# An expert unit for the first four batches' tokens, run in pieces between attention's last steps

## The chip, the cores and the metric

One core of one Trainium2 chip. The metric is device time in microseconds of one execution. TensorE (PE) multiplies, VectorE (DVE) does the top-k search and two-operand arithmetic, ScalarE (ACT) copies, exponentials and signs, GpSimd (POOL) additions and the indirect transfers, SyncE (SP) issues most of the other transfers. Each engine works through its own instructions in the order in which the program wrote them.

## The reference, cut to what matters

```python
scores = q @ k.T / 8                              # 8 batches x 8 heads, 576 x 576, head size 64
kth    = the 32nd largest score of each row
attn   = softmax(where(scores >= kth, scores, -1e9))
x      = (attn @ v) as 4608 tokens x 512          # all heads of a token side by side
e(n)   = argmax(x[n] @ w_gate)                    # one of 8 experts for each token
out[n] = prob(e(n)) * (relu(x[n] @ w1[e]) @ w2[e])  # 512 -> 1024 -> 512
```

## The kernel before

**Attention** runs in 144 steps (`steps`), a step being two 128-row slots of scores. The loop over `t` (lines 1004 to 1078) is a software pipeline: step t makes the scores of slot t+3 (`scores`, `scores_left`, PE and ACT, into the bank pair `MAINS` and one of seven SBUF buffers that `pair()` hands out), finds the top 32 of slot t (`topk`, lines 1025 and 1033, DVE: 21 first-level MAX8 and some 14 second-level operations), marks and adds (`softmax`, lines 454 and 455: ACT's sign, POOL's addition) slot t-2, transposes slot t-3 (`transp`, line 461), takes the exponential of slot t-4 (`exps`) and multiplies slot t-5 by the values (`av`, line 477). From t = 144 on the pipeline only empties; there are seven such steps.

**Side work** stands in lanes of generators (`j_sums`, `j_rows`, `j_find`, `j_redo`, `j_patch`, `j_route`): scaling and storing finished rows, repairing rows whose 32nd place is tied, and routing each batch's tokens into a table by expert. `advance` moves each lane by one `yield`; what a job emits goes into queues that are written out right after (DVE's at the next step, where the loop is still in attention). There is one `advance` in each attention step, one in each of the steps 144 to 148 (`TAIL`, `TADV = 5`, line 1061), and later one per expert layer (`drain(g)`, line 1425). A batch's chain is find, redo, patch, route, one `yield` after the other; the last batch's starts at t = 145.

**Experts.** An expert's tokens are worked in units of `T` tiles of 128 tokens. A unit has 8 layers `k` of 128 hidden values (`FC`). A layer is `hidden` (12 matmuls, line 1159, each operand split into a high and a low part, hence three products) and `project` (3 matmuls per tile, line 1174). Its weights (512 KB) are loaded by `raw_w` (lines 946 and 947) and split by `parts_w` into high (ACT line 954, DVE line 956) and low parts (DVE and POOL, line 957). A unit's tokens are gathered by `take` (line 876) and transposed and split by `turn_x` (line 1139 PE, 1140 ACT, 1141 DVE). `EARLY` names units that may run before all batches are routed: expert 0 with two tiles of tokens of the first five batches, experts 1 to 4 with three tiles of the first six. Then come experts 5 to 7 with five tiles each, what is left of experts 0 to 4 (three tiles, and four times two), and a spare tile. In `moe` step k, `fetch(u + 1)` gathers the next unit's tokens as soon as its batches are routed, and one tile is turned after each of a unit's layers 3 to 7. A unit whose tokens need all batches (`u >= first`) is fetched only once all lanes are empty, after which the counting of leftover tokens (`over`, lines 1242 to 1271) runs with a `moe` step between its parts.

**Around the border.** At t = 140 the first two layers' weights are loaded into the query and key buffers (`ahead_load`), at t = 145 unit 0's tokens are gathered (`ahead_take`), at t = 146 the two layers are split (`ahead_split`). All of unit 0's matmuls come after step 150.

Of the kernel before, what the change touches and what calls it, by code (L numbers as in the profile page):

```python
# [24 lines left out]
A0, A1, A2, A3 = -4, 1, 2, 2  # L25
EARLY = ((4, 1, 2), (3, 4, 3))
# [13 lines left out]
TADV = 5  # L40
# [8 lines left out]
def attention_moe(ctx, tc, q, k, v, w_gate, w1, w2, out):  # L49
    nc = tc.nc  # L50
# [738 lines left out]
    def j_route(b):  # L789
# [52 lines left out]
        for c in range(KB):  # L842
            if c == 0 or b not in ahead:
                yield need(pool=1.0)
# [104 lines left out]
    def parts_w(k, tiles):  # L949
        W[k] = []  # L950
        for i, r in enumerate(RAW.pop(k)):
# [5 lines left out]
            (nc.gpsimd if i else nc.vector).tensor_tensor(lo, r, hi, op=OP.subtract)  # L957
# [3 lines left out]
    def ahead_load(k):  # L961
        r = work.tile([128, MAIN, 4, D], F32, name=("rq", "rk")[k], bufs=1).rearrange("p i g d -> p (i g d)")
        raw_w(k, r[:, 0:DM], r[:, DM:2 * DM])

    def ahead_take():
        c, T = part_of[0]
        GX[0] = [jobs.tile([128, DM], F32, name="kt", bufs=4)[:, 0:DM] for _ in range(T)]
        for i in range(T):
            take(GX[0][i], ID[0][:, i, 0:1], c)

    def ahead_split(k):
        if k == 0:
            for i in range(2):
                t = jobs.tile([128, 2, VW], F32R, name=f"rv{(NQ + i) % NV}", bufs=1).rearrange("p g x -> p (g x)")
                SPARE.extend(t[:, c * DM:(c + 1) * DM] for c in range(2 * VW // DM))
            SPARE.extend(jobs.tile([128, DM], F32, name="kt", bufs=4).bitcast(F32R)[:, 0:DM] for _ in range(2))
        parts_w(k, [SPARE.pop(0) for _ in range(4)])

    SPARE = []
# [17 lines left out]
    if NQ > 1:  # L997
# [3 lines left out]
    AHEAD = [(A0, ahead_load, (0,)), (A0, ahead_load, (1,)), (A1, ahead_take, ()), (A2, ahead_split, (0,)),  # L1001
             (A3, ahead_split, (1,))]
    delayed = None
    for t in range(steps + LAG + TD + 4):
# [60 lines left out]
        for at, job, a in AHEAD if first else ():  # L1065
            if t - steps == at:
                job(*a)
# [14 lines left out]
    while first and part_of[0][0] not in ROUTED or held[0]:  # L1082
# [9 lines left out]
    late = {}  # L1092
    XP, HT, PY = {}, {}, {}
    outs = []

# [30 lines left out]

    def turn_x(u, t):
        T = units[u][2]
        if t >= T:
# [367 lines left out]
```

## Time and profile before

| | |
|---|---|
| median of 3 runs | 1301.82 us (1299.66 to 1303.17) |
| the profiled execution: its own time, its span | 1301.19 us, 1299.4 us |
| mean granted TensorE clock | 0.983 |
| busy PE, DVE, ACT, POOL | 1217.2, 1020.2, 828.3, 830.7 us |
| PE instructions, DVE instructions | 9126, 6889 |
| last top-k block ends, first expert layer begins | 760, 787.4 us |
| first five-tile unit begins | 969.7 us |

The page is read from the 40 slices of part 2: slices 1 to 23 are attention, in which DVE is at 9 tenths or more nearly throughout; slices 24 and 25 hold the border; from slice 26 on PE is at 9 nearly throughout and DVE falls to 3 to 7. "Granted clock" is TensorE's clock as a share of 2.4 GHz; it has two levels, so a share between one half and one is a mix over time of 1.2 and 2.4 GHz. Matmul ends are modelled, so that a busy PE need not be PE at its best.

### The profile page before, as it was taken

To read this page: it belongs to the slowest core of one execution; us is meant where nothing else is said; L and a number is where in the kernel's file an instruction comes from. 1 tells how busy PE (TensorE), PEld (TensorE's weight loads), DVE (VectorE), ACT (ScalarE), POOL (GpSimd) and SP (SyncE) were. 2 spreads that over 40 slices of the span, in tenths; PEclk is the share of its full clock that TensorE was granted. 3 is DMA by queue.
4 is the path that set the end of the run, shared out by engine and by line. 5 is a ranking of instruction groups with operands and counts; after the bars stand their busy time and mean duration, and the time that the engine had idled before them with its cause. 6 is when DMAs were issued, how large, how long until landed. Compare 5 with 4: busy or idle time off the path is not lost.

```text
span 1299.4 us, 31672 instructions
## 1 busy us (share of the span) xinstructions
PE 1217.2 (94%) x9126; PEld 968.9 (75%) x9126; DVE 1020.2 (79%) x6889; ACT 828.3 (64%) x1691; POOL 830.7 (64%) x1205
## 2 busy tenths in 40 slices
PE   6999999999999999999998869999999999999997
PEld 3667667676666666667666658889899899989996
DVE  7999999999999999999998965746663333345664
ACT  4999798898888888888987843333332323233432
POOL 4676766867867867868957866676552424155654
PEclk8999999999999999999999978999999999999999
DMA  6765565655655656556653615646563434256774
GB/s 174 224 184 178 169 187 161 186 171 160 193 161 156 195 168 171 179 170 171 188 166 113 194 39 159 187 122 199 146 184 110 125 93 132 74 162 189 224 212 125
DMA packets 271239, 211.18 MB, mean 163 GB/s; under 512 B 136216, under 2 KB 214216, under 8 KB 271056
## 3 DMA queue, kind: packets, MB, share of 16 engines
q1 hardware_dynamic: 260320, 185.92, 48.2%
q0 software_dynamic: 9504, 22.86, 5.6%
q8 instruction: 74, 1.21, 0.4%
q14 instruction: 109, 0.89, 0.2%
q10 hardware_dynamic: 1232, 0.30, 0.1%
HBM read 102.49 MB, written 107.90 MB: 162 GB/s over the span
## 4 chain that ended last, share of the span: by engine, by line
DVE 43%; PE 43%; ACT 4%; issue 3%; POOL 3%; DMA 2%; SPq 1%; POOLq 0%; ACTq 0%; DVEq 0%
DVE cand L1025 21%; PE ph L1159 18%; PE y L1174 17%; DVE cand L1033 9%; DVE vq L1033 7%; PE pt L265 2%; ACT sg L454 2%; POOL sb L455 2%; PE mt L1139 1%; PE ps L367 1%; PE px L477 1%; PE tt L461 1%; DVE xm L265 1%; ACT et L467 1%; DMA rk<-in_k_dram 1%
## 5 line engine op out<-in xcount | busy, mean ns | idle before, releaser
L455 POOL TENSOR_TENSOR sb<-sb,sg 128x576 f32<-128x576 f32 x288 | 369.4, 1299 | 49.4 <-ACT sg L454 42.3
L1025 DVE MAX8 cand<-sb 128x8 f32<-128x52 f32 (+2 forms) x3024 | 368.3, 207 | 0.2 <-issue 0.2
L957 POOL TENSOR_TENSOR wl<-r,wh 128x512 fp32r<-128x512 f32 x110 | 142.4, 1294 | 220.8 <-DVE wh L956 213.5
L454 ACT ACTIVATE sg<-sb,nb 128x576 int8<-128x576 f32 x288 | 229.0, 795 | 63.0 <-POOL sb L455 63.0
L477 PEld LDWEIGHTS px<-et,rv 128*64 128x64 f32 x2688 | 130.9, 138 | 123.1 <-ACT xt L265 49.4
L1160 ACT ACTIVATE hh<-ph 128x320 fp32r<-128x320 f32 (+3 forms) x136 | 58.2, 428 | 241.6 <-PE ph L1159 240.1
L1033 DVE MAX8 vq<-cand 128x8 f32<-128x22 f32 (+7 forms) x1152 | 200.5, 205 | 0.0
L461 PE MATMUL tt<-turner,sb 128*128 128x128 f32 x1296 | 176.8, 278 | 23.0 <-POOL sb L455 19.9
L367 PE MATMUL ps<-qk 64*128 64x512 f32 (+1 forms) x576 | 184.9, 650 | 4.2 <-ACT sb L369 3.5
L1161 DVE SCALAR_TENSOR_TENSOR hl<-ph,hh 128x320 fp32r<-128x320 f32 (+3 forms) x136 | 65.0, 478 | 151.3 <-ACT hh L1160 151.2
L467 ACT ACTIVATE et<-tt,shift 128x1152 f32<-128x1152 f32 x144 | 178.2, 1238 | 2.6 <-PE tt L461 2.6
L477 PE MATMUL px<-et,rv 128*64 128x128 f32 (+1 forms) x2688 | 164.3, 268 | 14.6 <-ACT xt L265 9.0
L461 PEld LDWEIGHTS tt<-turner,sb 128*128 128x128 f32 x1296 | 147.9, 144 | 34.7 <-POOL sb L455 30.2
L1159 PE MATMUL ph<-xh,wh 128*128 128x320 f32 (+3 forms) x536 | 168.5, 314 | 0.0
L1159 PE MATMUL ph<-xh,wl 128*128 128x320 f32 (+3 forms) x536 | 165.3, 308 | 0.0
L1159 PE MATMUL ph<-xl,wh 128*128 128x320 f32 (+3 forms) x536 | 165.1, 308 | 0.0
L1033 DVE MATCH_REPLACE8 cand<-vq,cand 128x22 f32<-128x22 f32 (+2 forms) x864 | 158.6, 189 | 0.0
L369 ACT ACTIVATE sb<-ps 128x1024 f32<-128x1024 f32 x144 | 149.0, 1035 | 9.4 <-PE ps L367 9.4
L1174 PE MATMUL y<-wh,hh 128*128 128x512 f32 x324 | 127.9, 395 | 1.9 <-ACT yo L1178 1.9
L1174 PE MATMUL y<-wh,hl 128*128 128x512 f32 x324 | 128.3, 396 | 0.0
L1174 PE MATMUL y<-wl,hh 128*128 128x512 f32 x324 | 128.1, 395 | 0.0
L957 DVE TENSOR_TENSOR wl<-r,wh 128x512 fp32r<-128x512 f32 x110 | 95.7, 870 | 11.4 <-ACT wh L954 7.1
(261 smaller groups left out, 2179.3 us busy)
## 6 DMA issues: line engine op xcount, KB each, us to landing
r<-in_moe_w_dram SPq DMA_DIRECT2D x220, 256.0 KB
sc<-sb SPq DMA_DIRECT2D x128, 288.0 KB
sc<-sb SPq DMA_DIRECT2D x128, 256.0 KB
rv<-in_v_dram SPq DMA_DIRECT2D x32, 256.0 KB
xs<-xm SPq DMA_DIRECT2D x16, 512.0 KB
rq<-in_q_dram SPq DMA_DIRECT2D x60, 128.0 KB
rk<-in_k_dram SPq DMA_DIRECT2D x60, 128.0 KB
sc<-sb SPq DMA_DIRECT2D x32, 144.0 KB
```

What stands on the lines that cost most here:

```text
L367: nc.tensor.matmul(MAINS[:, n], qk[:, 0, w], qk[:, 1, 2 * LEFT:], start=True, stop=True)
L369: nc.scalar.activation(bass.AP(EX[-1].tensor, EX[-1].offset, [list(EX[-1].ap[0]), [S + LEFT, 2], [1, M]]), MAINS, AF.Copy)
L454: nc.scalar.activation(upper(SG[i]), SB[u], AF.Sign, bias=nb[:, i, 1:2], accum_out=CNT[b][:, 2 * lt + i:2 * lt + i + 1])
L455: nc.gpsimd.tensor_tensor(SB[u], SB[u], SG[i], op=OP.add)
L461: nc.tensor.matmul(tt[:, c], x[:, c * 128:(c + 1) * 128], ident, start=True, stop=True, is_transpose=True)
L467: nc.scalar.activation(ET[t], three.rearrange("p (c q) -> p c q", c=NB9), AF.Exp, bias=shift[:, t // NT, 0:1], scale=0.125)
L477: yield lambda kb=kb, blk=blk: nc.tensor.matmul(px[h * 64:(h + 1) * 64], block(rv, p % 2, kb if kb < MAIN else MAIN + n, h), et[:, blk, q] ...
L957: (nc.gpsimd if i else nc.vector).tensor_tensor(lo, r, hi, op=OP.subtract)
L1025: one[m][0](*one[m][1])
L1033: f(*a)
L1159: nc.tensor.matmul(ph, a[:, c, :], x[:, c, s], start=(m == 0), stop=(m == len(seq) - 1))
L1174: nc.tensor.matmul(PY[u, t], a[:, s], x, start=(f == 0 and m == 0), stop=(f == FC - 1 and m == 2))
```

## The change

Expert 0's two-tile unit takes tokens of the first four batches instead of five; expert 1's early unit becomes a two-tile one with tokens of five batches, and its leftover unit a three-tile one. Unit 0 no longer runs in `moe`. A generator, `filler`, holds it in 20 pieces. One piece is taken at the end of each of the steps 139 to 143 and two in each of the steps 144 to 150, one ahead of `av` and one behind `transp`; the last after the loop. Weights come in eight 512 KB loads of two layers' w1 or two layers' w2 (`load`), into the query and key buffers in turn, and are split by ACT or DVE and DVE (`split`), 1024 elements per partition at a time, where the kernel before had 512. The splits lie in the three score-operand buffers, two value buffers and score buffers. `hid` uses `MAINS`, `out_of` accumulates all eight layers in it. Unit 1's tokens are gathered in step 149 (or when routed), turned after the loop in the transposes' bank, and its first layer's weights are loaded and split ahead. `moe` starts at unit 1. `advance` now also runs in steps 149 and 150.

```diff
-A0, A1, A2, A3 = -4, 1, 2, 2
-EARLY = ((4, 1, 2), (3, 4, 3))
+A0 = -5
+EARLY = ((5, 1, 2), (4, 1, 2), (3, 3, 3))
...
-TADV = 5
+TADV = 7
...
-            if c == 0 or b not in ahead:
+            if c == 0 or b not in ahead or b == part_of[0][0]:
                 yield need(pool=1.0)
...
+    def ahead_take(u, name, w):
+        c, T = part_of[u]
+        GX[u] = [jobs.tile([128, w], F32, name=name, bufs=4)[:, 0:DM] for _ in range(T)]
         for i in range(T):
-            take(GX[0][i], ID[0][:, i, 0:1], c)
+            take(GX[u][i], ID[u][:, i, 0:1], c)
...
+        def load(j):
+            r = raws[j] = raw(j)
...
+        def split(j):
+            hi, lo = sets[j % 3 if j < FC - 1 else 2]
+            r = raws.pop(j)
+            if j < FC // 2:
+                nc.scalar.activation(hi, r, AF.Copy)
+            else:
+                nc.vector.tensor_copy(hi, r)
+            nc.vector.tensor_tensor(lo, r, hi, op=OP.subtract)
+
+        def hid(k):
...
+            ph = MAINS[:, k % 2, 0:w]
+            seq = [(c, a, x) for c in range(DC) for a, x in ((h1, xh), (h1, xl), (l1, xh))]
+            for m, (c, a, x) in enumerate(seq):
+                nc.tensor.matmul(ph, a[:, c, :], x[:, c, :], start=(m == 0), stop=(m == len(seq) - 1))
+            nc.scalar.activation(hh, ph, AF.Relu)
+            nc.vector.scalar_tensor_tensor(hl_, ph, 0.0, hh, op0=OP.max, op1=OP.subtract)
...
+        load(0)
+        load(1)
+        yield
+        ahead_take(0, "kt", DM)
+        yield
...
+        split(0)
+        load(2)
+        XP[0] = [spare()[:, 0:DC * w].rearrange("p (c x) -> p c x", c=DC) for _ in range(2)]
+        for t in range(T):
+            turn_x(0, t, MAINS[:, t].rearrange("p (c x) -> p c x", c=DC))
+        yield
+        hid(0)
...
+        split(1)
+        load(3)
+        yield
+        hid(1)
+        sets.append((qs[2][:, 0:two], spare()[:, 0:two]))
+        split(2)
+        load(4)
+        yield
+        split(3)
+        load(5)
+        yield
+        for k in range(2, FC):
+            hid(k)
+            if k % 2:
+                split(4 + k // 2 - 1)
+                if k < FC - 1:
+                    load(6 + k // 2 - 1)
+                else:
+                    r = raw(0)
+                    raw_w(FC, r[:, 0:DM], r[:, DM:two])
+            yield
+        for k in range(FC - 1):
+            out_of(k)
+            if k == 3:
+                split(FC - 1)
+            if k == 4:
+                parts_w(FC, [jobs.tile([128, DM], F32, name="kt", bufs=4).bitcast(F32R) for _ in range(2)]
+                        + [t[:, two:two + DM] for t in rv], nc.vector)
+            if k >= 3 and 1 not in GX and part_of[1][0] in ROUTED:
+                ahead_take(1, "xt", S)
+            yield
...
+        for t in range(T):
+            turn_x(1, t, three[:, t * DM:(t + 1) * DM].rearrange("p (c x) -> p c x", c=DC))
+        out_of(FC - 1)
...
+        if t >= steps:
+            next(fills, None)
         if grp(t - LAG - TD - 2):
             av(t - LAG - TD - 2, grp(t - LAG - TD - 2))
...
             transp(t - LAG - TD)
+        if t >= steps:
+            next(fills, None)
...
+        if steps + A0 <= t < steps:
+            next(fills)
...
-    while first and part_of[0][0] not in ROUTED or held[0]:
+    while held[0] or next(fills, fills) is not fills:
...
-        for k in range(K):
+        load_w(FC + 1)
+        load_w(FC + 2)
+        for k in range(FC, K):
...
+            if k == FC:
+                split_w(k + 1)
             split_w(k + 2)
```

## Rows read from the trace of the kernel before

**Rows 1.** The page, part 2: busy tenths of VectorE and the granted clock of TensorE, in 40 slices of 32.5 us.

```profile
DVE  7999999999999999999998965746663333345664
...
PEclk8999999999999999999999978999999999999999
```

**Rows 2.** Busy time by stretch, from the ninth-last attention step to the first five-tile unit (us from the span's start: length, then busy us and instructions of each engine, granted clock, DMA share, GB/s); the last row sums 12 stretches that cover all of it without a gap.

```profile
735.30:757.00 21.70, 15.19 (x170) 12.20 (x171) 21.70 (x187) 16.02 (x29) 16.01 (x25) 1.00 0.40 127
757.00:762.40 5.40, 2.00 (x21) 1.36 (x19) 5.33 (x29) 1.71 (x7) 3.03 (x4) 0.74 0.04 10
762.40:774.90 12.50, 9.37 (x61) 8.38 (x61) 3.16 (x19) 5.73 (x11) 8.56 (x18) 0.64 0.32 88
774.90:785.60 10.70, 8.97 (x69) 6.61 (x67) 5.43 (x9) 3.39 (x6) 9.69 (x15) 0.92 0.19 42
...
787.40:794.90 7.50, 7.25 (x31) 6.66 (x32) 3.07 (x7) 1.81 (x4) 1.29 (x1) 0.58 0.47 140
...
917.30:925.20 7.90, 6.17 (x26) 5.56 (x25) 5.17 (x27) 1.61 (x3) 1.27 (x1) 0.78 0.30 77
...
sum 234.40, PE 215.00 PEld 189.64 DVE 151.07 ACT 89.77 POOL 148.55; mean PE 17.92 PEld 15.80 DVE 12.59 ACT 7.48 POOL 12.38
```

**Rows 3.** VectorE's instructions in order of time around the end of the last two top-k blocks (start, us, engine, line, what; in brackets the idle time before it and its releaser).

```profile
747.18 2.56 DVE L1025 MAX8 cand<-sb 128x8 f32<-128x52 f32 x21
...
753.69 2.56 DVE L1025 MAX8 cand<-sb 128x8 f32<-128x52 f32 x21
...
759.63 0.39 DVE L1033 MAX8 vq<-cand 128x8 f32<-128x88 f32 x2
...
760.50 1.22 DVE L265 TENSOR_TENSOR hist<-oh,valid 128x40 bf16<-128x40 f32 x1
```

**Rows 4.** TensorE's instructions in order of time from there to the first expert layer, those that it waited for.

```profile
761.77 0.23 PE L265 MATMUL pt<-hist,before 128*128 128x40 bf16 x1 [3.05 <-DVE hist L265]
...
770.45 1.97 PE L477 MATMUL px<-et,rv 128*64 128x128 f32 x16 [3.13 <-ACT r_et L265]
...
787.40 0.58 PE L1159 MATMUL ph<-xh,rv 128*128 128x256 f32 x1 [0.74 <-ACT xh L1140]
```

**Rows 5.** GpSimd's instructions in order of time, at attention's last steps.

```profile
743.26 0.28 POOL L265 IOTA pay<- 128x8 int32 x2
...
760.25 2.50 POOL L455 TENSOR_TENSOR sb<-sb,sg 128x576 f32<-128x576 f32 x2
...
770.95 1.09 POOL L876 DMA_INDIRECT kt<-xs,ids  x1 [0.16 <-issue]
```

**Rows 6.** The chain of waits late in the run, merged (start, us, what): one layer of a three-tile unit and one of a two-tile unit.

```profile
1174.20 2.09 PE ph L1159 x12
1176.29 2.10 PE y L1174 x9
...
1187.54 1.42 PE ph L1159 x12
1188.96 1.40 PE y L1174 x6
```

**Rows 7.** Single lines of code: operations by engine with the duration in ns, min/median/max, and the first and last start; then, from the DMA issues, the median us from issue to landing in the last column.

```profile
L957 DVE TENSOR_TENSOR wl<-r,wh x110: 680/693/2526, 791.9 to 1286.2; 128x512 fp32r<-128x512 f32 x110
L1140 ACT ACTIVATE xh<-mt x40: 582/599/602, 786.3 to 1261.1; 128x512 fp32r<-128x512 f32 x40
L1141 DVE TENSOR_TENSOR xl<-mt,xh x40: 677/692/695, 786.9 to 1261.8; 128x512 fp32r<-128x512 f32 x40
L1161 DVE SCALAR_TENSOR_TENSOR hl<-ph,hh x136: 276/492/558, 791.4 to 1289.8; 128x320 fp32r<-128x320 f32 x48, 128x256 fp32r<-128x256 f32 x40, 128x384 fp32r<-128x384 f32 x40, 128x128 fp32r<-128x128 f32 x8
gx<-xs,ids POOLq DMA_INDIRECT x39, 4.4
kt<-xs,ids POOLq DMA_INDIRECT x2, 3.4
```

**Rows 8.** VectorE and GpSimd in order of time, one moment at which both read two SBUF operands.

```profile
863.63 1.30 POOL L957 TENSOR_TENSOR wl<-r,wh 128x512 fp32r<-128x512 f32 x1
...
863.77 1.70 DVE L957 TENSOR_TENSOR wl<-r,wh 128x512 fp32r<-128x512 f32 x1
```

**Rows 9.** GpSimd in order of time at the end of routing: the last scatter to the table, a weight part, and the first gather of the five-tile unit.

```profile
914.61 0.92 POOL L847 DMA_INDIRECT table<-pay,pos  x1 [0.16 <-issue]
...
925.80 1.29 POOL L957 TENSOR_TENSOR wl<-r,wh 128x512 fp32r<-128x512 f32 x1 [7.06 <-DVE wh L956]
...
931.84 0.99 POOL L876 DMA_INDIRECT gx<-xs,ids  x1
```

**Rows 10.** TensorE there: the count of tokens (line 1441, as in rows 7), and the chain of waits (start, us, what): layer 29's two halves, the first transposes of the five-tile unit, its first layer.

```profile
L1441 PE MATMUL mt<-hist,ones x1: 174/174/174, 918.7 to 918.7; 128*128 128x8 bf16 x1
...
919.37 3.41 PE ph L1159 x12
922.78 2.42 PE y L1174 x9
...
950.74 0.44 PE mt L1139 x4
...
969.71 3.52 PE ph L1159 x24
```

**Rows 11.** TensorE in order of time: the one wait between the first unit and the second.

```profile
824.82 0.50 PE L1174 MATMUL y<-wh,hh 128*128 128x512 f32 x1 [1.91 <-ACT yo L1178]
```

More of the change, by code (lines that the diff above doesn't have):

```diff
@@ L956, in parts_w @@
                 nc.vector.tensor_copy(hi, r)
[L957 removed]
+            ((other or nc.gpsimd) if i else nc.vector).tensor_tensor(lo, r, hi, op=OP.subtract)
             W[k] += [w.rearrange("p (c f) -> p c f", c=DC) if i == 0 else w for w in (hi, lo)]
[L961 to L963 removed]
@@ L979, in attention_moe, with give, turn_x @@
-    SPARE = []
+    late = {}
+    XP, HT, PY = {}, {}, {}
+    outs = []
+    def give(u, t, y):
+        nc.gpsimd.memset(spacer, 0.0)
+        st = nc.gpsimd.indirect_dma_start(
+            out=out, out_offset=bass.IndirectOffsetOnAxis(ap=ID[u][:, t, 1:2], axis=0),
+            in_=y, in_offset=None, bounds_check=N - 1, oob_is_err=False)
+        for o in outs:
+            tc.declare_no_dep(st.ins, o.ins, reason="each token has a row of its own")
+        outs.append(st)
+    def turn_x(u, t, pt=None):
+        T = units[u][2]
+        if t >= T:
+            return
+        if u not in XP:
+            p = pool_of(u)
+            XP[u] = [p.tile([128, DC, T * 128], F32R, name=n, bufs=2) for n in ("xh", "xl2")]
+        xh, xl = XP[u]
+        s = slice(t * 128, (t + 1) * 128)
+        if pt is None:
+            pt = ps_a.tile([128, DC, 128], F32, name="mt")
+        for c in range(DC):
+            nc.tensor.transpose(pt[:, c, :], GX[u][t][:, c * 128:(c + 1) * 128], ident)
+        nc.scalar.activation(xh[:, :, s], pt, AF.Copy)
+        nc.vector.tensor_tensor(xl[:, :, s], pt, xh[:, :, s], op=OP.subtract)
@@ L1000, in attention_moe @@
     prep(2)
[L1001 to L1002 removed]
+    fills = filler()
     delayed = None
@@ L1125, in gather @@
             take(GX[u][t], ID[u][:, t, 0:1], part_of[u][0] if u < first else None)
-    def turn_x(u, t):
-        T = units[u][2]
-        if t >= T:
-            return
-        p = pool_of(u)
-        if t == 0:
-            XP[u] = [p.tile([128, DC, T * 128], F32R, name=n, bufs=2) for n in ("xh", "xl2")]
-        xh, xl = XP[u]
-        s = slice(t * 128, (t + 1) * 128)
-        pt = ps_a.tile([128, DC, 128], F32, name="mt") if u or not t else \
-            ps_a.tile([128, 512], F32, name="ph", bufs=2).rearrange("p (c x) -> p c x", c=DC)
-        for c in range(DC):
-            nc.tensor.transpose(pt[:, c, :], GX[u][t][:, c * 128:(c + 1) * 128], ident)
-        nc.scalar.activation(xh[:, :, s], pt, AF.Copy)
-        nc.vector.tensor_tensor(xl[:, :, s], pt, xh[:, :, s], op=OP.subtract)
     def hidden(k):
@@ L1178, in project @@
                 nc.scalar.activation(y, PY[u, t], AF.Copy, scale=ID[u][:, t, 2:3].bitcast(F32))
-                nc.gpsimd.memset(spacer, 0.0)
-                st = nc.gpsimd.indirect_dma_start(
-                    out=out, out_offset=bass.IndirectOffsetOnAxis(ap=ID[u][:, t, 1:2], axis=0),
-                    in_=y, in_offset=None, bounds_check=N - 1, oob_is_err=False)
-                for o in outs:
-                    tc.declare_no_dep(st.ins, o.ins, reason="each token has a row of its own")
-                outs.append(st)
+                give(u, t, y)
     def moe():
         K = len(units) * FC
-        got, turned = set(), set()
+        got, turned = {0, 1}, {0, 1}
         def fetch(u):
@@ L1194, in fetch @@
                 gather(u)
-        for k in range(2):
-            load_w(k)
-        while first == 0 and not late:
-            yield
-        if first:
-            got.add(0)
-        fetch(0)
-        load_w(2)
-        if not first:
-            split_w(0)
-            split_w(1)
-        for t in range(CT):
-            turn_x(0, t)
-        turned.add(0)
-        for k in range(K):
+        load_w(FC + 1)
+        load_w(FC + 2)
+        for k in range(FC, K):
             u, f = divmod(k, FC)
```

65 lines of the change are left out of this document (47 added, 18 removed).

## The prediction

> **What bounds the kernel now.** I read part 2 of the page first, then busy time by stretch around the border of attention and experts, then each engine in order of time there, last the chain of waits. VectorE is full until slice 22; behind the first slice TensorE's clock falls below nine tenths in two only, 24 and 25, at the border [rows 1]. In the expert part TensorE runs layer behind layer: a three-tile layer takes 2.09 + 2.10 = 4.19 us, a two-tile layer 1.42 + 1.40 = 2.82 us, with nothing between [rows 6]. So time can be won only where TensorE waits or runs at 1.2 GHz. From 735.3 us (step 139's multiplications) to the first five-tile layer at 969.7 us it is busy 215.0 of 234.4 us: 19.4 us of waiting [rows 2]. Busy time at less than full clock costs, as busy x (1 - clock), 0.5 + 3.4 + 0.7 + 3.0 + 1.4 = 9.0 us more (the stretches at 0.74, 0.64, 0.92, 0.58 and 0.78) [rows 2]. That is 28.4 us which a better order could win at most. The change moves no matmul away for good: unit 0 keeps 8 x 2.82 = 22.6 us, and the tile that expert 1's early unit loses (8 x 1.37 = 11.0 us) comes back in its leftover unit, at the same full pace, as both prices are read there [rows 6]. So the new time is the old one, minus 28.4, plus what TensorE will wait and lose to the clock in the new order.
>
> **Part by part, up to the histogram of batch 5.** In the steps 141 to 143 VectorE is the bound: one top-k block starts when the last ends, and TensorE, GpSimd and ScalarE have slack. After the last block (759.63 + 0.39 = 760.0 us) comes route's histogram at 760.50, for which TensorE waits until 761.77 [rows 3, 4]. All that `filler` puts on VectorE ahead of that histogram pushes it:
> - Step 141: the gather stands on GpSimd behind 743.26 + 0.28 = 743.5 us [rows 5]. Of two issues of 1.09 us with 0.16 us ahead of each the second starts at about 745.0 and lands 3.4 us later, at 748.4 [rows 5, 7]. The low parts of x are 0.69 us each [rows 7], behind a turn (0.44 [rows 10]) and a copy (0.60); with 0.4 us of hand-over the second ends at about 750.5. VectorE was free at 747.18 [rows 3] and works off `split(0)` meanwhile. The next block is late by 3.4 us, of which some 0.8 is standing still. Bounds: 2.6 (only the work) and 6 (a gather that lands 4.4 us after issue and a queue ahead of it).
> - `split`'s subtraction has 1024 elements per partition; the trace has 512 at 0.69 us [rows 7]. Bounds 0.69 and 1.39; I take 1.2. The low part of a two-tile hidden layer takes about 0.43 us (between the least, 0.28, and the median, 0.49) [rows 7]. Step 142 adds 0.43 + 1.2, the end of step 143 and step 144 add twice that: 4.9 us.
> - A subtraction of two SBUF operands that meets such an operation of GpSimd waits: 1.70 us instead of 0.69, the first having started 0.14 us after GpSimd's 1.30 us one [rows 8]. In these steps GpSimd does two additions of 1.25 us a step [rows 5], each set free by the end of a top-k block, just when the split comes. Between 0 and 1.25 us each; I take 0.75 for three: 2.2 us.
> - Batch 3 now ends its route with three small operations on VectorE that batches 4 and 5 alone had: about 0.5 us.
>
> The Trainium skill says the same of rows 8 (SBUF — State Buffer, "Who interferes with whom": one of the two blocks for the whole instruction of the other, whichever started first). It speaks against splitting on VectorE beside GpSimd's additions; without such a lock my sum would be 2.2 us less.
>
> The histogram's matmul so comes at 761.8 + 3.4 + 4.9 + 2.2 + 0.5 = 772.8 us. TensorE has until then 15.2 us of old work (its busy time in the first stretch of rows 2), 1.6 us of the second stretch's (2.00 less the two small matmuls behind the wait), 0.9 us of turning and three hidden layers at 1.42 us: 22.0 us. It waits 772.8 - 735.3 - 22.0 = **15.5 us** (bounds 12 and 20).
>
> **From there to unit 1.** Waiting behind the histogram are five hidden layers and eight output layers (18.3 us), what is left of attention and its side work, which now runs beside them, and two more rounds of `advance`. The waits of before in this stretch (3.13 us for r_et and 0.74 us for xh among them [rows 4]) are covered by these matmuls, whose weights' loads and splits run some 4 us ahead; if that cover fails, see the fourth rival. GpSimd loses here what it did before (two takes, two weight parts). TensorE comes out of a long wait: after the waits of 3.05 and 0.74 us it ran at 0.64 and 0.58 and lost 3.4 and 3.0 us [rows 2, 4]. I take **3.5 us** (bounds 0.5 and 6), and **0.5 us** for unit 1's last low part.
>
> **Unit 1.** Only its first layer is split ahead, before it was two. The loads of layers 9 and 10 go into the buffers that hold the last raw weights, so they are issued when unit 0's last splits are done, about 6 us before unit 1 starts, and the second layer's split comes behind the first layer's activation: ScalarE's and VectorE's part, some 1.3 us, plus a late load. **1.7 us** (0 and 5). The wait of 1.91 us between the first unit and the second [rows 11] I keep: **1.9 us**.
>
> **The last batch's chain.** This is where the moved steps are paid for. Attention's tail had 5 rounds of `advance`, the expert part 28 more until all lanes were empty: the count of tokens (918.7 us) stands directly before layer 29 (919.37) [rows 10]. The chain of batch 7 takes one round per `yield`, so 33 in all; now 7 come in the tail and 26 behind the first `moe` step, k = 8. The lanes are empty after k = 34; before it was after k = 28. The five-tile unit still starts at k = 40. Before, its gather was issued at 931.84, within layer 30, and first turned at 950.74, 19 us later [rows 9, 10]. Now the fetch falls to k = 35, and f = 3 there: the same `moe` step turns the first tile. The gather stands on GpSimd behind that step's weight part, which waits for VectorE's copy, which waits for the end of the projection. In layer 29, the same place: projection ends 922.78 + 2.42 = 925.20, weight part 925.80 + 1.29 = 927.09 [rows 9, 10], the gather would start at 927.3 and land 4.4 us later [rows 7], at 931.7. TensorE, in order, stands for **6.5 us** (bounds 5.5 and 8), and comes back at the lower clock, **3.0 us** (1.4, as after the shorter wait at 917.3 [rows 2], and 5). Behind the transposes wait the next layer's matmuls and all that follows. The count itself costs a wait of some **1.4 us** as before.
>
> **Sum.** 15.5 + 3.5 + 0.5 + 1.7 + 1.9 + 6.5 + 3.0 + 1.4 = 34.0 us against 28.4: **5.6 us slower**. The profiled execution took 1301.2 us; 1306.8, which is 5.0 above the median of the runs shown (1301.8). I forecast 1306.8 us, own range 1301 to 1313.
>
> At nothing I cost: the table's scatters (batch 3's spaced as they were, batch 4's in one go as they were); SP, whose loads wait for raw buffers ahead of the last rows' stores and of batch 5's slots, by some 10 us, while their readers come over 20 us later; the output scatters of unit 0, on GpSimd with slack.
>
> **Rivals.**
> 1. *The late fetch costs nothing* (18 in 100). If the lanes are empty a step or two earlier than I count, or the gather lands before TensorE gets there, 6.5 + 3.0 fall away: 24.5 against 28.4, 3.9 us faster, 1297.3. For it: a count by hand over four generators. Against: the same count gives 28 for the kernel before, which rows 10 show. It decides whether the kernel gains; the point is one `moe` step.
> 2. *VectorE's additions don't push* (18 in 100). If nothing collides (-2.2), the gather lands in time (-0.8), the splits cost 0.7 (-1.8) and the clock holds (-3.0), the late fetch as forecast: 34.0 - 7.8 = 26.2, 2.2 us faster, 1299, no difference that shows. For it: TensorE is busier here, which keeps its clock up. Against: VectorE's stretch has no gap.
> 3. *Both* (10 in 100): 34.0 - 9.5 - 7.8 = 16.7, 11.7 us faster, 1289.5. Then most of unit 0 lies beside attention's end and the chain keeps its lead.
> 4. *The pieces wait for their weights* (14 in 100). There are two raw buffers; a load can go only when the split two pieces earlier is done, and VectorE's copy for pieces 4 to 7 stands in its queue ahead of route's and rows' work. If each of these four loads comes 2.5 us late, TensorE loses 10 us more: 1316.8. For it: SP in order, its loads behind one another. Against: the transfer queues are nearly idle there (shares 0.04 to 0.32 [rows 2]).
>
> The forecast has 40 in 100. Repeated runs differ by 0.3%, 3.9 us, so "same" is 1297.9 to 1305.7. Of the forecast some 0.28 lie above, 0.12 within; with rival 4, slower 0.42; with rival 2 and a little of 1, same 0.30; the rest, faster, 0.28. The range 1292 to 1317 leaves out most of rival 3 and the upper part of rival 4.
>
> **What would show it.** In the trace after: the last top-k block ends near 766 us, TensorE's wait for the histogram is 5 to 10 us long, unit 1's first layer begins near 812 us; the count stands between layers 34 and 35, and the five-tile unit's first transposes wait 5 to 8 us for the gather. I am wrong if unit 1 begins before 803 us, or those transposes don't wait.

## The result and the profile after

The changed kernel takes 1314.21 us (median of four runs, 1313.54 to 1316.95), the kernel before beside it 1302.33 us: a ratio of 1.0099, with a 95% interval of 1.0078 to 1.012. It is 11.9 us slower by the medians, where 5.0 were forecast: 1.2 us above the range that I called my own (1301 to 1313), and inside the wider one (1292 to 1317). The profiled execution of the changed kernel took 1316.95 us (span 1314.8), 2.7 above its median, and its clock was the lowest of its runs (0.974); so of what follows some 3 us belong to this execution.

The page's part 2 of the kernel after, to be read beside [rows 1]: VectorE's busy tenths and TensorE's granted clock, in 40 slices of 32.9 us.

```profile
DVE  7999999999999999999998984645554333344665
...
PEclk8999999999999999999998889899899999999999
```

VectorE is at eight tenths in slice 24 (756 to 789 us), where it had six: the pieces' splits. The clock's dip, 7 and 8 in slices 24 and 25 before, is shallower and wider: 8 in slices 22 to 24, and again in 26 (expert 1's unit) and 29 (the late gather).

The same question as in [rows 2], asked of the kernel after, from the same multiplications (step 139, now at 735.97 us) to the first five-tile unit: length, busy us of each engine, granted clock, DMA share and GB/s of each stretch.

```profile
735.97:757.00 21.03, 12.91 (x104) 10.61 (x105) 19.20 (x135) 11.52 (x21) 15.59 (x25) 0.76 0.59 182
757.00:774.30 17.30, 13.35 (x132) 11.99 (x131) 17.05 (x88) 11.27 (x23) 9.78 (x8) 0.82 0.21 72
774.30:814.30 40.00, 38.13 (x261) 31.98 (x262) 19.06 (x45) 12.23 (x26) 21.62 (x35) 0.93 0.42 119
814.30:830.00 15.70, 13.22 (x89) 11.53 (x87) 10.01 (x18) 5.40 (x11) 12.25 (x17) 0.95 0.44 140
830.00:850.00 20.00, 15.30 (x88) 13.18 (x89) 13.23 (x34) 7.53 (x15) 10.99 (x16) 0.91 0.66 200
850.00:885.00 35.00, 35.00 (x178) 30.95 (x177) 16.55 (x34) 11.55 (x26) 22.80 (x33) 0.95 0.52 151
...
920.00:941.00 21.00, 20.11 (x102) 17.88 (x101) 10.88 (x23) 6.81 (x13) 14.32 (x21) 1.00 0.60 145
941.00:957.00 16.00, 8.37 (x27) 7.42 (x27) 6.32 (x27) 1.05 (x3) 7.02 (x7) 0.65 0.42 121
957.00:962.30 5.30, 5.30 (x23) 4.86 (x23) 2.95 (x10) 1.56 (x3) 1.14 (x2) 0.78 0.43 133
...
sum 240.63, PE 210.99 PEld 185.08 DVE 144.56 ACT 85.83 POOL 141.11; mean PE 19.18 PEld 16.83 DVE 13.14 ACT 7.80 POOL 12.83
```

TensorE's loss in a stretch is its length less its busy time, plus busy x (1 - clock). Row by row that gives:

| stretch | waiting + clock, us | forecast |
|---|---|---|
| step 139 to the histogram (735.97 to 774.3) | 8.1 + 3.1 and 4.0 + 2.4 = 17.6 | 15.5 |
| histogram to expert 1's unit (to 814.3) | 1.9 + 2.7 = 4.5 | 3.5 + 0.5 |
| expert 1's unit and the clock behind it (to 885) | 2.5 + 0.7, 4.7 + 1.4 and 1.8 = 11.0 | 1.7 + 1.9 |
| count and late gather (920 to 962.3) | 0.9, 7.6 + 2.9 and 1.2 = 12.6 | 6.5 + 3.0 + 1.4 |
| sum | 45.7 | 34.0 |

The stretch of before lost 28.4 [rows 2], so 17.3 us more are lost, where 5.6 were forecast. Of the 11.7 between them 7.4 are one line of the table, expert 1's unit, three times what I gave it; the others are 0.5 to 2.1 us too low. In whole: the stretch is 240.6 us long and was 234.4 (17.3 more loss, less the 11.0 us of the tile that moved away), what stands behind it is 8.5 us longer (338.45 us from the first five-tile layer to the end; 329.94 before), and the first multiplications come 0.7 us later. That is the 15.4 us between the two spans.

TensorE of the kernel after in order of time, the instructions whose waits make the first stretch (the bracket holds the idle time before an instruction, and its releaser); the fourth is the histogram's, as in [rows 4], and the last line is VectorE's part of it:

```profile
747.73 1.12 PE L986 MATMUL ps<-turner,kt 128*128 128x128 f32 x4 [4.46 <-DMA kt<-xs,ids]
750.86 1.11 PE L986 MATMUL ps<-turner,kt 128*128 128x128 f32 x4 [2.01 <-DVE sb L988]
768.84 2.93 PE L1037 MATMUL ps<-sb,rv 128*128 128x256 f32 x12 [1.31 <-DVE sb L1039]
773.67 0.24 PE L265 MATMUL pt<-hist,before 128*128 128x40 bf16 x1
```

```profile
773.20 0.33 DVE L265 TENSOR_TENSOR hist<-oh,valid 128x40 bf16<-128x40 f32 x1
```

The histogram's matmul was forecast for 772.8 and comes at 773.67 us. VectorE has the histogram ready at 773.53, pushed back as the sum had it, but TensorE has no wait for it any more: it arrives no earlier, having stood behind the gather and behind VectorE's low parts, the work queued ahead of it. Where I had expected one wait of 5 to 10 us there are several small ones.

At the other end, TensorE and GpSimd at the count and at the five-tile unit's gather (to be read beside [rows 9, 10]):

```profile
943.04 0.16 PE L1540 MATMUL mt<-lostb,ones 128*128 128x1 bf16 x1 [2.94 <-DVE lostb L1535]
955.84 1.08 PE L986 MATMUL mt<-turner,gx 128*128 128x128 f32 x4 [5.59 <-DMA gx<-xs,ids]
976.35 0.39 PE L1273 MATMUL ph<-xh,wh 128*128 128x320 f32 x1
```

```profile
950.85 1.26 POOL L957 TENSOR_TENSOR wl<-r,wh 128x512 fp32r<-128x512 f32 x1 [7.89 <-DVE wh L956]
952.26 0.98 POOL L876 DMA_INDIRECT gx<-xs,ids  x1
```

The count stands between layers 34 and 35 (layer 35 starts at 943.07), as the count of rounds said. The gather is issued behind the weight part, at 952.26, and the first transposes wait 5.59 us for it.

### The profile page after: what moved, and what is told of

Same layout as the page of the kernel before. It is cut to its first block, busy times and chain, and to the rows that moved or that the text cites. A ratio compares the mean times of both kernels' runs of the same rounds, so it can differ in the third digit from the quotient of the medians.

```text
span 1314.8 us, 31644 instructions
## 1 busy us (share of the span) xinstructions
PE 1222.3 (93%) x9127; PEld 974.6 (74%) x9127; DVE 1020.1 (78%) x6889; ACT 826.3 (63%) x1687; POOL 826.8 (63%) x1195
## 4 chain that ended last, share of the span: by engine, by line
DVE 46%; PE 36%; issue 5%; ACT 5%; POOL 5%; DMA 2%; SPq 1%; POOLq 0%; DVEq 0%; ACTq 0%
DVE cand L1160 22%; PE ph L1273 14%; PE y L1288 13%; DVE cand L1168 9%; DVE vq L1168 8%; POOL wl L957 2%; PE pt L265 2%; ACT sg L454 2%; PE ps L367 1%; DVE xm L265 1%; PE px L477 1%; PE mt L986 1%; PE ps L1037 1%; ACT sb L369 1%; ACT et L467 1%
## 5 line engine op out<-in xcount | busy, mean ns | idle before, releaser
L957 POOL TENSOR_TENSOR wl<-r,wh 128x512 fp32r<-128x512 f32 x103 | 133.7, 1298 | 225.2 <-DVE wh L956 220.2
L1275 DVE SCALAR_TENSOR_TENSOR hl<-ph,hh 128x320 fp32r<-128x320 f32 (+3 forms) x128 | 61.6, 481 | 149.8 <-ACT hh L1274 149.7
L1273 PE MATMUL ph<-xh,wh 128*128 128x320 f32 (+3 forms) x480 | 153.7, 320 | 0.0
L1273 PE MATMUL ph<-xh,wl 128*128 128x320 f32 (+3 forms) x480 | 150.7, 314 | 0.0
L1273 PE MATMUL ph<-xl,wh 128*128 128x320 f32 (+3 forms) x480 | 150.5, 313 | 0.0
L1288 PE MATMUL y<-wh,hl 128*128 128x512 f32 x310 | 122.3, 395 | 1.1 <-DVE hl L1275 1.1
L1288 PE MATMUL y<-wl,hh 128*128 128x512 f32 x310 | 122.3, 395 | 0.0
L1288 PE MATMUL y<-wh,hh 128*128 128x512 f32 x310 | 122.0, 394 | 0.0
L1273 PEld LDWEIGHTS ph<-xh,wh 128*128 128x128 f32 x480 | 91.6, 191 | 6.5 <-issue 3.7
```

Source lines behind the costliest of these rows:

```text
L957: ((other or nc.gpsimd) if i else nc.vector).tensor_tensor(lo, r, hi, op=OP.subtract)
L1273: nc.tensor.matmul(ph, a[:, c, :], x[:, c, s], start=(m == 0), stop=(m == len(seq) - 1))
L1288: nc.tensor.matmul(PY[u, t], a[:, s], x, start=(f == 0 and m == 0), stop=(f == FC - 1 and m == 2))
```

## The experiments

All times are medians; ratios are to the kernel before, run on the same chip in turn. In them the changed kernel stands at 1.0099, [1.0078, 1.012], and 0.001 is 1.3 us.

**The cut of the units alone.** The kernel before with the new cut, first without and then with the change's added condition on batch 3's scatters:

```
-EARLY = ((4, 1, 2), (3, 4, 3))
+EARLY = ((5, 1, 2), (4, 1, 2), (3, 3, 3))
...
-            if c == 0 or b not in ahead:
+            if c == 0 or b not in ahead or b == part_of[0][0]:
```

> The kernel before with the new cut of the units alone: unit 0 keeps two tiles, expert 1's early unit goes from three tiles to two, expert 2's from four to three, and the rest comes back in their leftover units; no pieces, the five-tile unit's chain as before. If the cut is neutral, as my sum took it (a tile moved keeps its price of 11.0 us), the time is that of before within 3 us. Rival: the cut itself costs what was lost, because a two-tile unit (a layer in 2.82 us) is too short for its weights' loads and splits: then 6 to 10 us slower than before, with waits of TensorE inside expert 1's unit.

> The kernel before with the new cut of the units, as in x1_cut_only, but with the change's added condition too, so that batch 3's scatters into the table stay spaced. In x1_cut_only attention came out some 4 us late: behind 595 us GpSimd issued the scatters in one go and its additions for the top-k came 5 us late. If that alone made x1 slower, this one is 4 us faster than x1, level with the kernel before within 2 us. Rival: the cut costs 4 us wherever it stands (the two-tile unit starves): then it stays 3 to 5 us slower than before, with attention on time and the loss behind 787 us.

Measured: without the condition 1306.86 us, ratio 1.0033 [1.0021, 1.0045]; with it 1302.73 us, ratio 1.0 [0.9988, 1.0012]. TensorE and GpSimd without the condition, around 600 us (the first and the last of five scatters to the table, which GpSimd issues in one go, and the additions behind them):

```profile
603.35 2.57 PE L461 MATMUL tt<-turner,sb 128*128 128x128 f32 x9 [4.99 <-POOL sb L455]
```

```profile
593.77 1.09 POOL L847 DMA_INDIRECT table<-pay,pos  x1 [2.41 <-DVE vq L1033]
...
599.14 0.91 POOL L847 DMA_INDIRECT table<-pay,pos  x1 [0.23 <-issue]
...
602.02 2.50 POOL L455 TENSOR_TENSOR sb<-sb,sg 128x576 f32<-128x576 f32 x2
```

So the cut is neutral, as the sum took it, and the one-line condition is worth 4 us: five scatters in one go put GpSimd's additions, and with them attention, 5 us back for good (where they are spaced, TensorE waits 0.88 us for the same additions). Of the cut itself the first expectation has one thing wrong: expert 2's early unit had three tiles before, and keeps them. The first run alone would have been read as its rival, a cut that costs. It also means that the whole loss of the changed kernel comes with the pieces, and that the kernel with the cut is the fairer one to compare stretches with. Its stretches, from step 139 to expert 2's unit and from there to the five-tile unit, in the view of before:

```profile
738.50:856.12 117.62, 99.23 (x704) 84.47 (x705) 83.87 (x333) 52.41 (x107) 80.39 (x118) 0.90 0.47 138
856.12:963.02 106.90, 105.18 (x551) 94.77 (x551) 69.11 (x158) 35.36 (x69) 65.88 (x84) 1.00 0.59 172
```

The changed kernel takes 113.7 us for the first (735.97 to 849.64) and 126.7 for the second (to 976.35). The pieces do win 4.0 us in front; they are paid for behind.

**The late gather.** A unit's first tile is turned only in a step behind the one that fetched it, and what is left over in the unit's last step:

```
+            had = u + 1 in got
             if f:
                 fetch(u + 1)
...
-            if u + 1 in got and f >= FC - CT:
+            if had and f >= FC - CT:
...
```

> The changed kernel, but a unit's first tile is turned only in a step behind the one that issues its gather. If the late gather is what my sum says, TensorE's wait of 5.6 us for it and about 3 us of clock behind it go, and about 1 to 2 us come back for two turns in the last step: 6 to 8 us faster than the changed kernel. Rival (the wait is hidden anyway, since what is gained there is lost by the weights behind it): within 2 us of the changed kernel.

Measured 1310.48 us, ratio 1.0062 [1.0046, 1.0077]: some 4 to 5 us won, under the 6 to 8 expected. The wait shrinks to 1.55 us, and the two tiles in the last step cost another 1.4.

The other way to the same wait, two rounds of side work in seven steps of expert 2's unit:

```
...
+                if 8 <= done < 15:
+                    for queue in (pq, aq, dq):
+                        flush(queue)
+                    advance(None)
+                    flush(gq)
+                done += 1
                 next(more)
```

> The changed kernel with two rounds of the side work instead of one in seven steps of expert 2's unit, so that the lanes are empty after layer 27, near where they were before (28). If the last batch's chain is late only because it lost seven rounds in attention's tail, the five-tile unit's gather is issued long before its first turn: the wait of 5.6 us and the slow clock behind it go, and the time falls by 6 to 9 us below the changed kernel's; the count's wait moves but stays. Rival: the rounds are bound by data (table, loads, the route's own chain) and not by their number; two rounds in a step then make TensorE wait for them in expert 2's unit, and less than 3 us is won.

Measured 1311.17 us, ratio 1.0067 [1.0046, 1.0087]. The wait for the gather is gone, and the count comes at layer 28. TensorE at the count:

```profile
918.20 0.16 PE L1547 MATMUL mt<-lostb,ones 128*128 128x1 bf16 x1 [1.39 <-DVE lostb L1542]
```

So the chain was late by the number of its rounds, as said, and not by its data. Two quite different edits win about the same 4 us, the second with a wide interval that still touches the changed kernel's: so much does the late gather cost in the median. The 6.5 + 3.0 of my sum is what the one profiled execution shows, with its clock.

**SyncE's queue.** In the changed kernel SyncE stood still for 11.0 us, from 822 to 833 us, in front of a load of route's slots (line 793), which waits for a scatter of GpSimd's. The weights' loads of expert 1's unit stand behind it. SyncE there, then ScalarE, which waits for the first of these weights:

```profile
833.40 0.33 SPq L793 DMA_DIRECT2D ll<-lps  x1
...
834.35 0.53 SPq L946 DMA_DIRECT2D r<-in_moe_w_dram  x1
```

```profile
837.64 0.63 ACT L954 ACTIVATE wh<-r 128x512 fp32r<-128x512 f32 x1 [3.87 <-DMA r<-in_moe_w_dram]
```

I took this for the cause of the unit's waits, and moved the two loads to GpSimd's queue once attention is over:

```
-        nc.sync.dma_start(ll[:, 0:MAIN], lps...
+        (nc.sync if att_open[0] else nc.gpsimd).dma_start(ll[:, 0:MAIN], lps...
...
```

> The changed kernel, but behind attention's end the two loads of route's slots go through GpSimd's queue and not through SyncE's, so that the weights' loads don't stand behind them while they wait for the table's scatters. If the hole of some 11 us in SyncE's queue (822 to 833 us) starves expert 1's unit, TensorE's waits and low clock between 814 and 850 us fall from 11 us to 4 or less: 5 to 8 us faster than the changed kernel. Rival: the two-tile unit starves because only its first layers are loaded ahead and GpSimd is late with its parts: then within 2 us of the changed kernel, with waits of the same size.

Measured 1315.01 us, ratio 1.0097 [1.0081, 1.0114]: nothing. The load has left SyncE's queue, and expert 1's unit still takes 34.45 us (35.40 in the changed kernel). TensorE in that unit with the loads moved:

```profile
831.37 0.70 PE L986 MATMUL mt<-turner,gx 128*128 128x128 f32 x4 [2.88 <-DMA gx<-xs,ids]
...
847.44 0.50 PE L1288 MATMUL y<-wh,hl 128*128 128x512 f32 x1 [1.56 <-DVE hl L1275]
```

As the whole cause that theory fell, but not as a link: the changed kernel's longest wait in this unit, 3.01 us for VectorE's `xl`, does go back to the late load (`xl` stands behind a low part that waits for ScalarE's copy at 837.64), and with the loads moved, the weights go out from 822.40 on and that wait is gone. Others grew in its place: 2.88 us for the gather (1.58 in the changed kernel) and 2.3 for `hl` (1.1). SyncE's own waiting moved too: it then stood 6.5 us for GpSimd's low part, which frees the raw buffer.

**GpSimd in expert 1's unit.** What is left is GpSimd, which between 815 and 837 us has unit 0's output scatters, unit 2's gather, the next batch's route and the weights' low parts one behind the other. In this one the low parts go to VectorE, for this unit alone:

```
-            parts_w(k, [moe_a.tile([128, DM], F32R, name=n, bufs=3) for n in ("wh0", "wl0", "wh1", "wl1")])
+            parts_w(k, [moe_a.tile([128, DM], F32R, name=n, bufs=3) for n in ("wh0", "wl0", "wh1", "wl1")],
+                    nc.vector if k < 2 * FC else None)
```

> The changed kernel, but the low part of the second weight of expert 1's early layers is subtracted on VectorE, not on GpSimd. New theory, since freeing SyncE's queue gave nothing: between 815 and 837 us GpSimd is full (scatters of output, gathers, the route of the next batch), its low parts come late, and the raw buffers with them. If so, expert 1's unit shrinks from 35 us to 30 or less: 3 to 6 us faster than the changed kernel. Rival (the loads' own time from issue to landing, or the gather for the next unit, sets the pace): within 1.5 us of the changed kernel, and the unit's first transposes still wait for the gather.

Measured 1311.17 us, ratio 1.0067 [1.005, 1.0083], an interval that still touches the changed kernel's. The unit in the changed kernel with the loads moved, and here (two kernels, the same view: length, busy us, clock, DMA share, GB/s; GpSimd's is the fifth busy time):

```profile
814.68:849.13 34.45, 27.76 (x174) 23.65 (x175) 24.92 (x52) 13.44 (x28) 24.80 (x34) 0.95 0.60 180
```

```profile
815.55:847.34 31.79, 26.24 (x175) 22.23 (x175) 24.77 (x59) 13.32 (x28) 16.20 (x25) 0.99 0.65 197
```

GpSimd is busy 16.2 us instead of 24.8, the wait for unit 2's gather is gone, and the unit is 2.7 us shorter than there and 3.6 than in the changed kernel. What is left of the waits is 5.6 us, 4.1 of them on VectorE's low parts. The first of these, 1.8 us, still goes back to a weights' load behind the slots' load, for part of what was won came through SyncE too: with less to do GpSimd scatters the route's slots earlier, and SyncE issues their load 15.1 us into the unit (830.61) instead of 19.2. Both edits together, this one and the moved loads, were not run. The lesson of the miss: GpSimd's low parts were never named by TensorE's waits (they say gather, xl, hl, wh); they only stood behind them.

**Both.**

> x2_turn_later and x8_unit1_vec together. If the late gather and GpSimd's load in expert 1's unit are separate costs, the gains add: 7 to 10 us faster than the changed kernel, some 1 to 4 us behind the kernel before. Rival: what is gained in expert 1's unit is lost at the next one, which waits for the route's chain all the same: then it is level with x2_turn_later within 1.5 us.

Measured 1307.23 us, ratio 1.0038 [1.0026, 1.005]: 0.0061 below the changed kernel, where the two alone won 0.0037 and 0.0032. Within their intervals they add up, so they are separate costs.

**The push in front.** Two runs on what VectorE does ahead of the histogram. In the first the pieces begin two steps later:

```
-A0 = -5
+A0 = -3
```

> The changed kernel with the pieces begun two of attention's steps later, so that VectorE does little of them ahead of batch 5's histogram. My theory of the push: the histogram's matmul comes 8 to 10 us earlier (near 764 us by the clock of the profile), but as much of unit 0 lies behind attention, so the time gains little: 0 to 4 us faster than the changed kernel. Rival (VectorE's push is the main cost of the change): 8 us faster or more. Other side: the pieces' rounds stand longer behind attention and TensorE waits for them: slower by 3 us or more.

Measured 1312.44 us, ratio 1.0073 [1.0057, 1.0088]. TensorE in front:

```profile
761.79 1.12 PE L986 MATMUL ps<-turner,kt 128*128 128x128 f32 x4 [6.99 <-DVE sb L988]
...
775.18 0.23 PE L265 MATMUL pt<-hist,before 128*128 128x40 bf16 x1 [2.49 <-DVE hist L265]
```

The histogram comes 39.6 us behind step 139's multiplications, later than in the changed kernel (37.7): the low part that TensorE waits for stands behind a whole top-k block (753.69 to 760.0), and the rest still lies ahead of the histogram. So this run did not take the push away, as both theories had assumed. What it won comes from the other end: three more rounds run behind attention, and no turn waits for the late gather. Up to expert 2's unit it takes 118.1 us (113.7 in the changed kernel), from there to the five-tile unit 116.2 (126.7). In the second run the low parts of the first four pieces go to GpSimd:

```
-            nc.vector.tensor_tensor(lo, r, hi, op=OP.subtract)
+            (nc.gpsimd if j < 4 else nc.vector).tensor_tensor(lo, r, hi, op=OP.subtract)
```

> The changed kernel, but the pieces' first four low parts (1024 elements, ahead of attention's end) are subtracted on GpSimd, not on VectorE. If VectorE's push is what holds the histogram, as my sum has it (1.2 to 2.6 us for each), the histogram's matmul comes 4 to 7 us earlier than in the changed kernel and the time falls by 3 to 6 us. Rival: GpSimd's additions for the top-k come late behind 2.6 us subtractions and VectorE waits for them instead: no gain or up to 5 us slower.

Measured 1316.49 us, ratio 1.0108 [1.0091, 1.0125]: no gain. GpSimd, VectorE and TensorE there:

```profile
766.34 2.38 POOL L1024 TENSOR_TENSOR sb<-rq,qk 128x1024 fp32r<-128x1024 f32 x1
```

```profile
766.54 2.24 DVE L265 SCALAR_TENSOR_TENSOR oh<-sh,edesc 128x40 f32<-128x40 f32 x1
```

```profile
770.21 2.80 PE L1037 MATMUL ps<-sb,rv 128*128 128x256 f32 x12 [1.75 <-DVE sb L1039]
```

VectorE is rid of four subtractions (7.4 us in the changed kernel), but a small operation of the route, of 40 elements, now takes 2.24 us beside GpSimd's subtraction (0.18 in the changed kernel), and the one ahead of it 0.84 (0.19). The low part behind them comes late, TensorE waits 1.75 us for it (1.31 in the changed kernel), and the histogram comes 1.4 us later than there (39.1 us behind step 139). The rival holds in its result, no gain, though not quite by the way it said: 2.7 us of what VectorE gave away came back to it as collisions, and the rest went in waiting. How much the push costs in all stays open, since neither run removed it.

**The front's gather a step earlier.**

```
-A0 = -5
+A0 = -6
...
         ahead_take(0, "kt", DM)
         yield
+        yield
```

> The changed kernel with the pieces' loads and gather one attention step earlier, splits and turns where they are. The turn of the first tile no longer waits 4.5 us for the gather. By my sum (0.8 us of VectorE standing still) the histogram comes about 1 us earlier and the time falls by 0 to 2 us. Rival: VectorE's block behind that turn is what the whole front waits for, then 3 to 5 us are won. Other side: the gather's 1.1 us issues on GpSimd come ahead of its additions for the top-k and push VectorE: up to 2 us slower.

Measured 1318.44 us, ratio 1.0123 [1.0101, 1.0145]: slower, by something that neither theory held. TensorE and SyncE there, and SyncE in the changed kernel:

```profile
743.61 1.98 PE L477 MATMUL px<-et,rv 128*64 128x128 f32 x16 [6.04 <-DMA rv<-in_v_dram]
```

```profile
735.53 0.40 SPq L1010 DMA_DIRECT2D rq<-in_moe_w_dram  x1
...
736.58 0.51 SPq L291 DMA_DIRECT2D rv<-in_v_dram  x1
```

```profile
732.89 0.43 SPq L291 DMA_DIRECT2D rv<-in_v_dram  x1
...
738.51 0.39 SPq L1010 DMA_DIRECT2D rq<-in_moe_w_dram  x1
```

The pieces' weights now stand ahead of attention's last values on SyncE, and attention waits 6 us for these. The wait for the gather (4.5 us) is gone, and from those multiplications on the run takes 573.9 us (575.5 in the one with the slots' loads moved); that doesn't make up for it.

**All together.** With the earlier gather, and then without it:

> x10_late_vec with two rounds a step as in x11_two_rounds and the gather a step earlier as in x12_take_early. If the costs are separate (expert 1's parts on GpSimd 3 to 4 us, the late gather with its turns 5 to 8, the front's gather 0 to 2), the sum is 9 to 13 us below the changed kernel: between 1302 and 1306 us, level with the kernel before or up to 3 us behind it. Rival (the costs share one cause): no better than x10_late_vec, 1307 us.

> x13_all without the earlier gather, which there held up a load of attention's values by 5 us: the late turn, expert 1's parts on VectorE, and two rounds of the side work a step. From the multiplications of step 139 on, x13_all took 564 us, the kernel before 564, x10_late_vec 568. If the three costs (late gather, GpSimd in expert 1's unit, rounds lost in attention's tail) are what the change paid, this one is level with the kernel before within 3 us, some 10 us below the changed kernel and 2 to 4 below x10_late_vec. Rival: x13's gain came from the earlier gather; then it stays at x10_late_vec's 1307 us.

Measured: 1309.2 us, ratio 1.0065 [1.0049, 1.0081], with the same wait for values (5.08 us); and without it 1305.64 us, ratio 1.0034 [1.0023, 1.0045]. The last is 8.5 us below the changed kernel by the ratios, and 4.4 us behind the kernel before, so not level as I had expected; it is no better than both fixes without the rounds (1.0038), since the rounds and the later turn cure one and the same wait. No version here beats the kernel before. The three edits' stretches, step 139 to expert 1's unit, that unit, from there to the five-tile unit, and the rest:

```profile
736.31:812.84 76.53, 61.13 (x493) 51.38 (x493) 54.47 (x257) 34.35 (x70) 45.88 (x65) 0.91 0.45 127
812.84:844.67 31.83, 26.44 (x174) 22.46 (x175) 24.78 (x59) 13.33 (x28) 16.27 (x25) 0.98 0.67 197
844.67:963.00 118.33, 113.75 (x589) 101.17 (x589) 76.25 (x171) 37.63 (x74) 70.65 (x94) 0.99 0.54 157
963.00:1301.50 338.50, 329.92 (x1928) 299.58 (x1926) 149.15 (x261) 110.28 (x221) 150.05 (x154) 0.99 0.48 144
```

The third stretch is still 11.4 us longer than with the cut alone (106.9). 8.6 us of that is busy TensorE, 7.7 of it the side work's matmuls (tile `pt`: 8.14 us, 0.44 with the cut alone), which the cut alone does ahead of expert 2's unit. That is work moved, not lost, and most of the 9.3 us won up to that unit (108.4 against 117.6) consists of it: 7.9 us of `pt` are gone from there. TensorE doesn't wait less: 20.8 us against 18.4 up to expert 2's unit, and 4.6 against 1.7 behind it. What is truly won in front is clock: at 0.93 (over 87.6 us busy) instead of 0.90 (over 99.2) it loses some 4 us less. From step 139 on this execution, 2.1 us below its median, is 2.2 us longer than the one with the cut alone (565.2 and 563.0); that is what of the 4.4 us the rows show, and the rest is not placed. So the pieces fill the border with one kind of work and push another kind out behind it.

## Why the prediction was right and wrong

- **Direction and reason: right.** Slower, because a better-filled border is bought with side work that comes later; but less waiting the pieces did not bring: up to expert 2's unit TensorE waits 21.1 us, and 18.4 with the cut alone. The 28.4 us at stake, the tile that only moves, the count of rounds (34) and the place of the late gather are as written.
- **The signs.** Three of five came as written: unit 1 near 812 us (814.2), the count between layers 34 and 35, the transposes' wait (5.59 us). The last top-k block ends at 768.5, not near 766, and the wait of 5 to 10 us for the histogram is not there.
- **Up to the histogram: nearly right** (17.6 against 15.5). The forecast's 772.8 us was met within 1 us (773.67), in a run whose step 139 came 0.7 us later. But its 15.5 counted waiting alone; the trace shows 12.1 us of waiting and 5.5 of slow clock. The first term was too small: in step 141 VectorE's next block is late by 5.7 us (747.54 to 753.24), not 3.4 and a collision; other terms were a little too large.
- **VectorE and GpSimd meeting: right in size.** I took 2.2 us. VectorE of the kernel after, the subtractions of 1024 elements, then GpSimd's additions beside them:

```profile
747.54 2.65 DVE L1024 TENSOR_TENSOR qk<-rq,qk 128x1024 fp32r<-128x1024 f32 x1
...
761.01 1.22 DVE L1024 TENSOR_TENSOR rv<-rk,rv 128x1024 fp32r<-128x1024 f32 x1
...
769.84 2.30 DVE L1024 TENSOR_TENSOR qk<-rk,qk 128x1024 fp32r<-128x1024 f32 x1
```

```profile
746.59 2.51 POOL L455 TENSOR_TENSOR sb<-sb,sg 128x576 f32<-128x576 f32 x2
...
761.09 3.53 POOL L455 TENSOR_TENSOR sb<-sb,sg 128x576 f32<-128x576 f32 x2 [0.18 <-ACT sg L454]
...
768.71 4.58 POOL L455 TENSOR_TENSOR sb<-sb,sg 128x576 f32<-128x576 f32 x2
```

  1.22 us alone (I took 1.2), 2.65 and 2.30 where GpSimd's addition had begun first: 1.4 + 1.1 = 2.5 us more. Where VectorE began first, GpSimd paid instead: its pair of additions at 761.09 took 3.53 us, not 2.5, and the pair at 768.71 took 4.58. The Trainium skill's rule (SBUF — State Buffer, "Who interferes with whom"), that one of the two is held for the whole instruction of the other, whichever started first, agrees with the rows from 761 us on. At 747.54 VectorE lost 1.4 us where only some 0.3 were left of the addition under way, so it seems to have stood through the next addition too, which started behind it.
- **Histogram to expert 1's unit: right** (4.5 against 4.0; the unit begins at 814.24, forecast 812).
- **Expert 1's unit: the step that failed.** I took 1.7 us for the second layer's weights, plus 1.9 for the boundary: 3.6, where 11.0 were lost, with the clock behind it. I priced one late weight and kept the rest at full pace, since the price of a two-tile layer (2.82 us) came from the end of the run [rows 6], where nothing else happens. Here its eight layers took 35.4 us, of which TensorE was busy 28.2 (the layers, three turns and side work), and it waited on four things in turn:

```profile
817.59 0.51 PE L1273 MATMUL ph<-rv,wh 128*128 128x256 f32 x2 [0.99 <-ACT wh L954]
...
830.32 0.65 PE L986 MATMUL mt<-turner,gx 128*128 128x128 f32 x4 [1.58 <-DMA gx<-xs,ids]
...
839.99 1.12 PE L986 MATMUL mt<-turner,gx 128*128 128x128 f32 x4 [3.01 <-DVE xl L988]
...
847.95 0.50 PE L1288 MATMUL y<-wh,hl 128*128 128x512 f32 x1 [1.11 <-DVE hl L1275]
```

  The sum put two things at nothing, and the waits came through both. GpSimd "with slack": the output scatters wait 3.97 us for their tile, until 815.45, and then the next batch's route stands ahead of a low part and of unit 2's gather (822.1 to 825.4). And SyncE: its weights' loads stood behind the slots' load, and ScalarE waits 3.87 us for one. Taking GpSimd's parts away won 4.2 us by the ratios. The wait between the units, which I kept at 1.9, did not come. With the cut alone it does, at 2.66 us for the same copy of ScalarE's as in [rows 11], with 0.69 us for `hl` beside it; so the other waits in this unit came with the pieces.
- **The late gather: right in mechanism and place** (5.59 us, forecast 6.5). In the median it costs 4 to 5, less than the 9.5 with its clock. The count's wait was 2.94, not 1.4.
- **The tile's move: 2.5 us off the other way.** It was to add 11.0 us behind the first five-tile layer, and added 8.5.
- **Rivals.** That the late fetch, or VectorE's additions, cost nothing is refuted by the rows. The fourth, that pieces wait for their weights, did not happen in unit 0 (TensorE waits 1.9 us in 40 there); its mechanism turned up one unit later. That its price, 10 us, was near what I had missed in all (11.7) is chance: it was reckoned for another unit.

## What to carry to other kernels

Price moved work in the place it moves to: a layer's time from a quiet end of the run is a floor, and a smaller unit leaves every other engine less time per layer for the same weights and the same side work. When rounds of a hand-ordered schedule are taken from one place, count where the last of them now falls, and what stood just behind it. And the engine that TensorE's waits name is often only the last link: moving a wait of 11 us out of SyncE's queue won nothing, because other waits grew in its place, and moving work off GpSimd, whose low parts TensorE never waited for by name, won 4 us.

## What was not expected of the hardware

- Five scatters issued back to back kept GpSimd from 593.77 to 600.05 us, 1.26 us each, and delayed attention by 5 us, which it never made up. The same wait of 4.7 us (TensorE for GpSimd's additions) stands near 700 us in the kernel before and in the one after, where batch 4's scatters go out in one go. Spacing them was not tried.
- Behind the first five-tile layer every kernel with the new cut takes 338.4 to 338.9 us, where the sum gave 340.9. In the changed kernel the layers there are a little shorter: most two-tile layers take 2.76 us instead of 2.82, and the 24 five-tile layers 171.5 us instead of 172.9. With 24 two-tile layers that is 1.4 + 1.4 us, about the 2.5 by which the moved tile came cheaper. The granted clock is 0.99 in both; the cause was not looked for.
